# Block attention with a gated MLP: another order for the first 60 steps, and two tiles' low parts on another engine

## The chip, the core and the metric

The kernel runs on one core of one Trainium2 chip. The metric is the device time of one execution in microseconds (us), the median of several runs. A core has a matrix engine (TensorE, PE in the rows; its weight loads are PEld), a vector engine (VectorE, DVE), an engine for activation functions (ScalarE, ACT), a general engine (GpSimd, POOL) and SyncE (SP), which here issues the DMA transfers. Each engine works through its own instructions in order; semaphores tie the engines together.

## What is computed

There are 8 batches of 576 tokens, 8 heads of width 64. Attention stays inside chunks of 64 tokens. Its result, laid out as 512 features for each token, goes into an MLP whose second half of hidden features is normalised, mixed over the tokens by a 576x576 matrix and multiplied onto the first half:

```python
scores = scale * np.matmul(q_c, k_c.transpose(0, 1, 2, 4, 3))      # chunks of 64 tokens
attn = np.exp(scores - max); attn = attn / (sum + 1e-09)
x = np.matmul(attn, v_c)                                           # -> (8, 576, 512)
h = gelu_tanh(x @ w_in)                                            # 512 -> 1024
u, v = h[..., :512], h[..., 512:]
v_n = (v - mean) / np.sqrt(var + 1e-06) * g_ln
v_s = np.einsum('ts,bsd->btd', w_sg, v_n) + b_sg[None, :, None]
out = x + (u * v_s) @ w_out
```

## The kernel before

**Numbers in two parts.** The MLP's products are taken as high part times high part plus the two cross terms, so each operand of the MLP exists as a high and a low tile: `xh`/`xl` for x, `win_h`/`win_l` for w_in, and so on. An element of w_in arrives as a 64-bit word and has to be turned into such a pair on the chip. `pair_begin` does the first half on ScalarE and VectorE: one ScalarE pass (L130) and five VectorE passes (L131, L132, L133, L162, L166) for 512 columns. `pair_end` does the second half: ScalarE writes the high part (L174), four TensorE products with small diagonal matrices add up what is left in PSUM (L178), and ScalarE writes the low part (L179). w_in has eight such parts: four for the v columns (one for each 128 input features) and four for the u columns. The loads of the u parts go into the same staging tiles as the v parts', so `v_w_end` issues each of them when its v part is done.

**Attention tiles.** The 4608 tokens are 36 tiles of 128 rows. A tile is loaded (`att_load`), its scores are made on TensorE (L314 for tiles 0 to 4, L322 for later ones), VectorE takes the maxima (L333), then either ScalarE makes the exponentials head by head with the maximum as its bias (L344, tiles 0, 2 and 4) or VectorE subtracts and ScalarE makes one pass (L346, L349). The sums are inverted on VectorE (L356, L357) and multiplied on (L358): on VectorE for the first batches' tiles, but on GpSimd where the step's name, here `n2`, stands in the table `ON_POOL`. The first five tiles are transposed on TensorE (L366) and copied out by ScalarE (L368); the product with V is L398. `keep` then writes that result into `xf`, `xh` and `xl`. For a tile whose name (`l0` to `l3`) is in `ON_POOL`, ScalarE copies PSUM to `xf` (L428), casts `xf` to `xh` (L94), and GpSimd subtracts (L97). For any other tile ScalarE casts PSUM to `xh`, VectorE subtracts from PSUM (L97), and ScalarE copies `xf` last (L432). For the first tile of a batch 64 of its rows are copied once more into `xodd` (L438).

**MLP units.** For a batch, `v_unit` (L452, 12 matmuls of 512 columns; five units for two batches together, four otherwise), four `u_unit` (L489), four `s_unit` (the mixing over tokens, L509) and four `o_unit` (L532) follow each other. After the first two batches they run in a fixed loop, with the attention of the next batch put into slots between them.

**The order of the start.** Everything up to the end of batch 1 is written in the string `START` (L46 to L50), one word a step: A loads tiles up to a number, S, T and O are a tile's scores, transpose and product (P and Q two tiles at once), L, W and w load, begin and end a v part of w_in, X and x begin and end a u part, M and G load other constants, g splits w_sg, v, u, s and o are the units (v03 is unit 3 of batch 0), and D with a number makes that many spare matmuls (`keep_clock`, L577) that nothing uses. The framework's scheduler sets each engine's queue from this program order and from the dependencies, so a queue is close to the order of the string but not the same word for word. PSUM has three tiles for scores, units and parts (`ps_m`) and two banks which the transposes and products of the first tiles take in turn (`next_bank`).

Of the kernel before, what the change touches and what calls it, by code (L numbers as in the profile page):

```python
# [42 lines left out]


START = """
L0 A0 A1 L1 S0 L2 T0 D11 A2 W0 A3 W1 L3 A4 S1 W2 S2 w0 w1 W3 T1 O0 w2 S3 O1 T2 w3 D14 O2 T3 S4 M0 v00 X0 O3 G0 T4 v01  # L46
A8 O4 x0 X1 v02 x1 X2 v03 X3 v04 u00 x2 g0 g1 u01 x3 g2 g3 u02 P5 g4 u03 T5 s00 T6 P7 s01 Q5 s02 T7 T8 s03 Q7 v10 v11
Y0 v12 Y1 v13 Y2 u10 Y3 u11 Y4 u12 Y5 Y6 u13 Y7 A10 s10 A12 s11 P9 s12 s13 T9 o00 T10 P11 o01 o02 o03 Q9 A14 T11 o10
T12 o11 Q11 S13 A15 o12 T13 o13
"""  # L50

PE_TILES = 5
# [9 lines left out]
}  # L62


ON_POOL = ("l0", "l1", "l2", "l3", "n2")
ACT_SOFTMAX = (0, 2, 4)


# [12 lines left out]
def block_attention_gated_mlp(ctx: ExitStack, tc: tile.TileContext, qkv, w_in, w_out, w_sg, g_ln, b_sg, out):  # L81
# [41 lines left out]
    def pick(step):  # L123
        return nc.gpsimd if step in ON_POOL else nc.vector

# [292 lines left out]
    def keep(t, xo):  # L418
        for b, at, off, n in segments(t):
# [6 lines left out]
            dst = [a[b][:, :, off : off + n].rearrange("p hp (c s) -> p c hp s", s=D) for a in (xh, xl, xf)]  # L426
            if f"l{t}" in ON_POOL:
                nc.scalar.copy(dst[2], src)  # L428
# [208 lines left out]
```

## Time and profile before

| what | value |
|---|---|
| median of 3 runs (lowest, highest) | 514.78 us (514.69, 514.84) |
| the profiled execution's own time | 516.12 us |
| its span, from first to last instruction | 514.3 us |
| mean granted TensorE clock | 0.996 of full |
| TensorE busy | 500.4 us, 97% of the span |
| VectorE, ScalarE, GpSimd busy | 337.0, 274.4, 73.7 us |
| TensorE in the chain that ended last | 83% of the span |

The profile is one execution. Its busy times tell how full an engine is, and its chain follows the last instruction back through whatever released it. A single share over 514 us hides that the start works under other limits than the rest: in the first 40th of the span TensorE is busy at 5 tenths, in nearly all later ones at 9 or more. So the first 70 us are read instruction by instruction, in the timeline.

### The profile page before, as it was taken

How to read it: one execution, taken by the hardware profiler on the slowest of the kernel's cores; microseconds unless marked ns; L12 is line 12 of the kernel's file. 1: busy time of each engine (PE TensorE's matmuls, PEld its weight loads, DVE VectorE, ACT ScalarE, POOL GpSimd, SP SyncE). 2: the span in 40 equal slices, each digit the busy share in tenths (PEclk: the TensorE clock that was granted, in tenths of full speed). 3: DMA queues.
4: the chain of work that ended last, by engine and by line, in shares of the span. 5: the costliest groups of instructions: out<-in, count | busy, mean ns of one | idle time of the engine just before them, and what ended most of it. 6: DMA issues, size and time to landing. Idle time of an engine off the chain costs nothing.

```text
span 514.3 us, 12454 instructions
## 1 busy us (share of the span) xinstructions
PE 500.4 (97%) x5273; PEld 464.8 (90%) x5278; DVE 337.0 (66%) x704; ACT 274.4 (53%) x509; POOL 73.7 (14%) x75
## 2 busy tenths in 40 slices
PE   5989999899999999999999999999999999999997
PEld 5677899699999899998999899998999899998996
DVE  5978759986866875577465686578456685536042
ACT  5788667853435865345643666345644666334210
POOL 0033300020110231013100140013100140102000
PEclk9999999899999999999999999999999999999999
DMA  8776001216438404060406304060406200020002
GB/s 333 271 217 198 0 1 43 70 38 174 114 113 222 138 1 126 24 193 2 124 4 190 87 0 126 24 192 2 124 1 193 86 0 3 14 81 0 1 1 92
DMA packets 49595, 46.58 MB, mean 91 GB/s; under 512 B 35202, under 2 KB 39554, under 8 KB 49540
## 3 DMA queue, kind: packets, MB, share of 16 engines
q1 hardware_dynamic: 49540, 45.80, 29.5%
q8 instruction: 41, 0.67, 0.5%
q14 instruction: 14, 0.11, 0.1%
HBM read 36.34 MB, written 9.44 MB: 89 GB/s over the span
## 4 chain that ended last, share of the span: by engine, by line
PE 83%; DVE 6%; ACT 5%; POOL 2%; issue 2%; DMA 1%; DVEq 0%; SPq 0%; POOLq 0%; ACTq 0%
PE pm L509 21%; PE pm L532 19%; PE pm L489 19%; PE pm L452 17%; PE pm L410 3%; PE banks L322 3%; POOL sm L461 1%; PE pm L577 1%; DMA qkv_t<-qkv 1%; DVE nmax L333 1%; PE pm L314 1%; ACT ptT L380 1%; ACT ptT L375 1%; POOL xl L97 1%; ACT pt L344 0%
## 5 line engine op out<-in xcount | busy, mean ns | idle before, releaser
L509 PE MATMUL pm<-wsg,v 128*128 128x288 f32 x768 | 108.0, 296 | 0.0
L509 PEld LDWEIGHTS pm<-wsg,v 128*128 128x128 f32 x768 | 103.9, 189 | 0.4
L532 PE MATMUL pm<-gh,wout 128*128 128x288 f32 x512 | 92.3, 297 | 0.0
L532 PEld LDWEIGHTS pm<-gh,wout 128*128 128x128 f32 x512 | 76.1, 189 | 0.5
L358 POOL TENSOR_TENSOR pt<-pt,den 128x512 f32<-128x512 f32 x28 | 30.8, 1112 | 226.3 <-DVE den L357 151.3
L461 POOL TENSOR_TENSOR sm<-sm,neg_half 128x1 f32<-128x1 f32 x36 | 36.3, 1008 | 160.4 <-DVE sm L460 120.1
L489 PE MATMUL pm<-xh,win_l 128*128 128x288 f32 x256 | 55.4, 298 | 0.7 <-ACT win_l L179 0.7
L532 PE MATMUL pm<-gl,wout 128*128 128x288 f32 x256 | 55.4, 296 | 0.0
L94 ACT CAST gh<-gt 128x576 fp32r<-128x576 f32 x32 | 21.5, 673 | 62.8 <-DVE gt L513 62.7
L489 PE MATMUL pm<-xh,win_h 128*128 128x288 f32 x256 | 55.0, 296 | 0.0
L489 PE MATMUL pm<-xl,win_h 128*128 128x288 f32 x256 | 55.0, 296 | 0.0
L452 PE MATMUL pm<-win_h,xl 128*128 128x512 f32 x128 | 52.0, 407 | 0.0
L452 PE MATMUL pm<-win_l,xh 128*128 128x512 f32 x128 | 51.2, 400 | 0.0
L452 PE MATMUL pm<-win_h,xh 128*128 128x512 f32 x128 | 51.1, 399 | 0.0
L513 DVE TENSOR_TENSOR gt<-pm,u 128x576 f32<-128x576 f32 x32 | 24.2, 756 | 40.2 <-PE pm L509 40.2
L540 DVE TENSOR_TENSOR ot<-pm,xf 128x576 f32<-128x576 f32 (+1 forms) x33 | 24.1, 733 | 29.8 <-PE pm L532 29.8
L489 PEld LDWEIGHTS pm<-xh,win_l 128*128 128x128 f32 x256 | 41.4, 188 | 2.2 <-ACT win_l L179 1.2
L532 PEld LDWEIGHTS pm<-gl,wout 128*128 128x128 f32 x256 | 41.5, 189 | 0.0
L489 PEld LDWEIGHTS pm<-xl,win_h 128*128 128x128 f32 x256 | 41.1, 188 | 0.0
L489 PEld LDWEIGHTS pm<-xh,win_h 128*128 128x128 f32 x256 | 41.0, 188 | 0.0
L97 DVE TENSOR_TENSOR xl<-pm,xh 128x512 fp32r<-128x512 f32 (+1 forms) x34 | 21.8, 640 | 26.2 <-ACT xh L94 26.2
L458 DVE BATCH_NORM_STATS2 sm<-hs 128x6 f32<-128x512 f32 x36 | 24.8, 688 | 19.6 <-ACT hs L455 19.4
(121 smaller groups left out, 830.8 us busy)
## 6 DMA issues: line engine op xcount, KB each, us to landing
qkv_t<-qkv SPq DMA_DIRECT2D x32, 512.0 KB, 4.5
out_dram<-ot SPq DMA_DIRECT2D x31, 288.0 KB, 2.2
qkv_t<-qkv SPq DMA_DIRECT2D x124, 64.0 KB, 3.6
qkv_t<-qkv SPq DMA_DIRECT2D x3, 768.0 KB, 9.7
wsg<-w_in SPq DMA_DIRECT2D x4, 512.0 KB, 5.2
wout<-w_in SPq DMA_DIRECT2D x4, 512.0 KB
st<-w_out SPq DMA_DIRECT2D x8, 256.0 KB, 3.1
stage<-w_sg SPq DMA_DIRECT2D x5, 288.0 KB, 3.6
```

Of the source, the lines that this page charges most:

```text
L94: nc.scalar.copy(hi, src)
L97: lo_eng.tensor_tensor(lo, src, hi.bitcast(F32), op=ALU.subtract)
L322: nc.tensor.matmul(sc[o, c, h // 2, :], qt[r, 0, h, :], qt[r, 1, h, :], start=True, stop=True)
L358: (nc.gpsimd if t > last[1] else pick(f"n{t}")).tensor_tensor(pt, pt, den.unsqueeze(2).broadcast_to([P, H, D]), op=ALU.mult)
L452: nc.tensor.matmul(pv, a[:, kt, tok], c[:, kt, DH:], start=(i == 0), stop=(i == 11))
L458: nc.vector.bn_stats(st, h)
L461: nc.gpsimd.tensor_tensor(rs, rs, neg_half, op=ALU.pow)
L489: nc.tensor.matmul(pm[:, j, :HS], a[:, kt, dc], c[:, kt, j * HS : (j + 1) * HS], start=(i == 0), stop=(i == 11))
L509: nc.tensor.matmul(pm[:, j, :HS], a[:, dc], c[:, m, j * HS : (j + 1) * HS], start=(i == 0), stop=(i == len(ops) - 1))
L513: nc.vector.tensor_tensor(gt.rearrange("p (a c) -> p a c", a=2), pm[:, :, :HS], u2[0][:, dt, :].rearrange("p (a c) -> p a c", a=2), op=ALU ...
L532: nc.tensor.matmul(pm[:, j, :HS], a[:, kt, ec], c[:, kt, j * HS : (j + 1) * HS], start=(i == 0), stop=(i == len(ops) - 1),)
L540: nc.vector.tensor_tensor(ot[:, js], pm[:, js, :HS], res[:, js], op=ALU.add)
```

## The change

The string `START` is written anew in its first third, and three names leave `ON_POOL`; nothing else is touched.

```diff
 START = """
-L0 A0 A1 L1 S0 L2 T0 D11 A2 W0 A3 W1 L3 A4 S1 W2 S2 w0 w1 W3 T1 O0 w2 S3 O1 T2 w3 D14 O2 T3 S4 M0 v00 X0 O3 G0 T4 v01
-A8 O4 x0 X1 v02 x1 X2 v03 X3 v04 u00 x2 g0 g1 u01 x3 g2 g3 u02 P5 g4 u03 T5 s00 T6 P7 s01 Q5 s02 T7 T8 s03 Q7 v10 v11
+L0 A0 L1 A1 L2 L3 A4 W0 S0 W1 D8 w0 S1 W2 T0 w1 S2 O0 T1 W3 w2 S3 O1 T2 M0 w3 S4 O2 T3 v00 X0 O3 G0 T4 v01 x0 X1 O4 A8
+v02 x1 X2 v03 X3 v04 u00 x2 g0 g1 u01 x3 g2 g3 u02 P5 g4 u03 T5 s00 T6 P7 s01 Q5 s02 T7 T8 s03 Q7 v10 v11 Y0 v12 Y1
...
-ON_POOL = ("l0", "l1", "l2", "l3", "n2")
+ON_POOL = ("l0", "l1")
```

The loads of the v parts 1 to 3 (L1, L2, L3) are issued ahead of those of tiles 2 to 4 (before, part 3 came behind tile 3). The v parts are begun and ended earlier between the tiles' steps. Of the spare matmuls 8 stay of 25: D11 becomes D8, D14 goes. Units v00 and v01 keep their words but stand differently to the steps around them. The low parts of tiles 2 and 3, and the multiplication that ends the softmax of tile 2, move from GpSimd to VectorE. From the gelu of u01 on, every engine's queue is the same as before.

On TensorE, from the first scores on, before (`qkv_t_108` and `qkv_t_111` are tiles 0 and 1, `wsg_0_106` is the staging tile of v part 0):

```order
L314 MATMUL pm_115<-qkv_t_108 64x64 x16
L577 MATMUL pm_156<-ident_84 128x128 x11
L314 MATMUL pm_188<-qkv_t_111 64x64 x16
L366 MATMUL banks_105<-ident_84,pt_134 128x128 x4
L314 MATMUL pm_221<-qkv_t_168 64x64 x16
L178 MATMUL pm_254<-wsg_0_106,ident_84 128x512
```

and now (`qkv_t_113` is tile 1, `wsg_1_111` is v part 1):

```order
L314 MATMUL pm_131<-qkv_t_108 64x64 x16
L577 MATMUL pm_170<-ident_84 128x128 x8
L178 MATMUL pm_179<-wsg_0_106,ident_84 128x512
L178 LDWEIGHTS low_0_86
L178 MATMUL pm_179<-wsg_0_106,low_0_86 128x512
L178 LDWEIGHTS low_1_87
L178 MATMUL pm_179<-wsg_0_106,low_1_87 128x512
L178 MATMUL pm_179<-win_h_90,ident_84 128x512
L314 MATMUL pm_188<-qkv_t_113 64x64 x16
L366 MATMUL banks_105<-ident_84,pt_150 128x128 x4
L178 MATMUL pm_227<-wsg_1_111,ident_84 128x512
```

Three spare matmuls are gone, and part 0's four products stand in front of the scores of tile 1; part 1's follow the transpose of tile 0.

On TensorE just ahead of the first matmul of v00 (L452), before (`pt_240` is tile 2, `pt_338` tile 3, `qkv_t_168` tile 2, `qkv_t_186` tile 4):

```order
L577 MATMUL pm_380<-ident_84 128x128 x5
L366 MATMUL banks_105<-ident_84,pt_240 128x128 x4
L577 MATMUL pm_380<-ident_84 128x128 x9
L398 MATMUL banks_105<-ptT_369,qkv_t_168 64x64 x16
L314 MATMUL pm_420<-qkv_t_186 64x64 x15
L366 MATMUL banks_105<-ident_84,pt_338 128x128 x4
L314 MATMUL pm_420<-qkv_t_186 64x64
L452 MATMUL pm_454<-win_h_90,xl_302 128x512
```

and now (`pt_255` is tile 2, `qkv_t_123` tile 4, `wout_1_117` part 3):

```order
L178 MATMUL pm_369<-wout_1_117,low_1_87 128x512
L314 MATMUL pm_378<-qkv_t_123 64x64 x13
L366 MATMUL banks_105<-ident_84,pt_255 128x128 x4
L314 MATMUL pm_378<-qkv_t_123 64x64 x3
L178 MATMUL pm_369<-win_h_90,ident_84 128x512
L452 MATMUL pm_436<-win_h_90,xl_287 128x512
L452 MATMUL pm_436<-win_l_91,xh_286 128x512
L398 MATMUL banks_105<-ptT_366,qkv_t_119 64x64 x16
```

The fourteen spare matmuls are gone, v00 begins in front of the product of tile 2 (the last row), and the transpose of tile 3 has moved into v01.

On ScalarE around the exponentials of tile 2, before (`pt_240`, in L344) with part 3's high part behind them (`wout_1_184`):

```order
L368 COPY ptT_282<-banks_105 128x512
L344 ACTIVATE pt_240,den_241<-pm_221,nmax_238 128x64 x8
L428 COPY xf_300<-banks_105 128x2x4x64
L179 ACTIVATE win_l_91<-pm_310 128x512
L94 CAST xh_301<-xf_300 128x2x4x64
L174 ACTIVATE win_h_90<-wout_1_184 128x512
L438 CAST xodd_0_306<-xh_301 128x4x64
L438 CAST xodd_1_307<-xl_302 128x4x64
L349 ACTIVATE pt_338<-pt_338 128x512
L428 COPY xf_300<-banks_105 128x2x4x64
L179 ACTIVATE win_l_91<-pm_371 128x512
```

and now (`pt_255` is tile 2, `pt_335` tile 3):

```order
L174 ACTIVATE win_h_90<-wout_0_115 128x512
L428 COPY xf_285<-banks_105 128x2x4x64
L94 CAST xh_286<-xf_285 128x2x4x64
L438 CAST xodd_0_291<-xh_286 128x4x64
L179 ACTIVATE win_l_91<-pm_307 128x512
L438 CAST xodd_1_292<-xl_287 128x4x64
L368 COPY ptT_299<-banks_105 128x512
L344 ACTIVATE pt_255,den_256<-pm_236,nmax_253 128x64 x8
L428 COPY xf_285<-banks_105 128x2x4x64
L349 ACTIVATE pt_335<-pt_335 128x512
L94 CAST xh_286<-xf_285 128x2x4x64
```

The copies and casts of tile 0 and its wait for `xl` have moved in front of tile 2's exponentials; the copy of tile 1 (`xf_285`, second time) follows directly behind them.

## Rows read from the trace of the kernel before

**Rows 1.** Stretches: us, PE, PEld, DVE, ACT, POOL busy, granted clock, DMA, GB/s.

```profile
15.00:20.00 5.00, 4.60 (x18) 2.10 (x15) 5.00 (x13) 3.52 (x6) 0.00 (x0) 1.00 0.77 279
20.00:25.00 5.00, 5.00 (x82) 3.28 (x83) 4.85 (x12) 4.58 (x21) 0.33 (x1) 1.00 0.65 196
```

**Rows 2.** Chain that ended last, first 35 us: start, us, engine, tile, line.

```profile
5.74 1.98 PE pm L314 x32
7.71 4.64 PE pm L577 x22
12.35 1.10 PE pm L314 x32
13.48 0.69 DVE nmax L333
...
24.67 1.04 POOL pt L358
25.71 1.25 POOL xl L97
```

**Rows 3.** Timeline of PE: start, us, instruction; in brackets idle before, and releaser.

```profile
28.54 0.63 PE L366 MATMUL banks<-ident,pt 128*128 128x128 f32 x4 [0.82 <-ACT xf L428]
...
29.00 2.17 PE L577 MATMUL pm<-ident 128*128 128x128 f32 x18
...
34.66 0.50 PE L452 MATMUL pm<-win_h,xl 128*128 128x512 f32 x1
...
65.06 0.53 PE L489 MATMUL pm<-xh,win_l 128*128 128x288 f32 x2 [0.74 <-ACT win_l L179]
```

**Rows 4.** Timeline of PE: part ends, a product, v and u units.

```profile
15.03 1.12 PE L178 MATMUL pm<-wsg,ident 128*128 128x512 f32 x2
...
16.66 1.02 PE L178 MATMUL pm<-wsg,ident 128*128 128x512 f32 x2
...
24.66 1.15 PE L398 MATMUL banks<-ptT,qkv_t 64*64 64x64 f32 x32
...
44.77 0.40 PE L452 MATMUL pm<-win_h,xl 128*128 128x512 f32 x1
...
47.57 1.02 PE L178 MATMUL pm<-wsg,ident 128*128 128x512 f32 x2
...
59.43 0.43 PE L489 MATMUL pm<-xh,win_l 128*128 128x288 f32 x2
...
62.62 1.02 PE L178 MATMUL pm<-wout,ident 128*128 128x512 f32 x2
```

**Rows 5.** Timeline of DVE and ACT: softmax of tiles 1, 2, part 3.

```profile
18.62 0.68 DVE L358 TENSOR_TENSOR pt<-pt,den 128x512 f32<-128x512 f32 x1
...
20.83 0.42 DVE L131 TENSOR_SCALAR wout<-wout 128x512 f32<-128x512 f32 x1
20.95 0.31 ACT L344 ACTIVATE pt<-pm,nmax 128x64 f32<-128x64 f32 x1
...
22.93 0.69 DVE L166 SCALAR_TENSOR_TENSOR wout<-wout 128x512 uint16<-128x512 uint16 x1
...
23.29 0.62 ACT L428 COPY xf<-banks 128x512 f32<-128x512 f32 x1
```

**Rows 6.** Timeline: POOL and DVE side by side, then DVE alone.

```profile
42.23 1.53 POOL L97 TENSOR_TENSOR xl<-xf,xh 128x512 fp32r<-128x512 f32 x1 [6.44 <-ACT xh L94]
...
42.60 1.70 DVE L467 SCALAR_TENSOR_TENSOR hs<-hs,sm,g_bc 128x512 f32<-128x512 f32 x1
...
48.05 0.74 DVE L467 SCALAR_TENSOR_TENSOR hs<-hs,sm,g_bc 128x512 f32<-128x512 f32 x1
```

**Rows 7.** Timeline of PE, and one stretch (columns of Rows 1).

```profile
81.65 1.16 PE L410 MATMUL pm<-ptT,qkv_t 64*64 64x64 f32 x64
...
91.94 1.94 PE L410 MATMUL pm<-ptT,qkv_t 64*64 64x64 f32 x64 [1.47 <-ACT ptT L380]
...
95.00:96.00 1.00, 1.00 (x4) 0.81 (x3) 1.00 (x4) 0.27 (x1) 0.00 (x0) 0.50 0.82 250
```

More of the change, by code (lines that the diff above doesn't have):

```diff
@@ L45 @@
 START = """
-L0 A0 A1 L1 S0 L2 T0 D11 A2 W0 A3 W1 L3 A4 S1 W2 S2 w0 w1 W3 T1 O0 w2 S3 O1 T2 w3 D14 O2 T3 S4 M0 v00 X0 O3 G0 T4 v01
-A8 O4 x0 X1 v02 x1 X2 v03 X3 v04 u00 x2 g0 g1 u01 x3 g2 g3 u02 P5 g4 u03 T5 s00 T6 P7 s01 Q5 s02 T7 T8 s03 Q7 v10 v11
-Y0 v12 Y1 v13 Y2 u10 Y3 u11 Y4 u12 Y5 Y6 u13 Y7 A10 s10 A12 s11 P9 s12 s13 T9 o00 T10 P11 o01 o02 o03 Q9 A14 T11 o10
-T12 o11 Q11 S13 A15 o12 T13 o13
+L0 A0 L1 A1 L2 L3 A4 W0 S0 W1 D8 w0 S1 W2 T0 w1 S2 O0 T1 W3 w2 S3 O1 T2 M0 w3 S4 O2 T3 v00 X0 O3 G0 T4 v01 x0 X1 O4 A8
+v02 x1 X2 v03 X3 v04 u00 x2 g0 g1 u01 x3 g2 g3 u02 P5 g4 u03 T5 s00 T6 P7 s01 Q5 s02 T7 T8 s03 Q7 v10 v11 Y0 v12 Y1
+v13 Y2 u10 Y3 u11 Y4 u12 Y5 Y6 u13 Y7 A10 s10 A12 s11 P9 s12 s13 T9 o00 T10 P11 o01 o02 o03 Q9 A14 T11 o10 T12 o11 Q11
+S13 A15 o12 T13 o13
 """
```

## The prediction, made before the changed kernel ran

> **What bounds the kernel now.** I read the stretches first. From 15 to 25 us VectorE is busy for 9.85 of 10 us [rows 1]: the start is bound by the softmax of the first tiles and the making of w_in's parts, both of which pass through VectorE. The chain of waits says the same with more detail. It runs through the 22 spare passes (4.64 us) into the scores of tile 1, from their end at 13.45 into VectorE (the maxima at 13.48), and about eleven us later into GpSimd, which does tile 2's multiplication and then the low part of tile 0 [rows 2]. Next I read TensorE's own timeline. The transpose of tile 2 waits until 28.54 for ScalarE, 18 more spare passes take 2.17 us behind it, and the first matmul of v00 starts at 34.66 [rows 3]. From there TensorE is nearly full, up to a last wait of 0.74 us at 65.06, the first matmul of u02 [rows 3]; from u01 on all queues are the same in both kernels. So the question is only when u02 starts: 65.06 us now. What comes behind is carried along, and 1 us earlier there is 1 us less of time.
>
> **Prices.** The end of a weight part takes TensorE 1.63 us (16.66 less 15.03), a product of one tile 1.15, a v unit 2.80 (47.57 less 44.77), a u unit 3.19 (62.62 less 59.43) [rows 4]; a transpose is 0.63 [rows 3], scores 1.10 [rows 2]. From tile 1's maxima at 13.48 [rows 2] to the end of its multiplication at 19.30 [rows 5] VectorE needs 5.82 us, with seven steps of weight parts between. The five VectorE steps of one part take 2.79 (20.83 to 23.62), and the exponentials of tile 2 keep ScalarE 2.34 (20.95 to 23.29) [rows 5]. A low part costs GpSimd 1.25 at the least [rows 2] and 1.53 at most [rows 6].
>
> **The change, step by step, up to v00.**
> 1. D11 to D8. Scores of tile 0 end at 7.71 as before. 22 passes in 4.64 us are 0.21 each; 16 are 3.37, so they end at 11.1 in place of 12.35: a gain of 1.25.
> 2. Part 0 ends in front of tile 1's scores: 1.63 more, and some 0.4 of it because TensorE is still slow there (0.21 us a pass, against 0.12 for the 18 later ones; tile 0's scores 1.98, tile 1's 1.10 [rows 2, 3]). So these scores run from 13.1 to 14.2, against 13.45 now: a loss of 0.75. In return VectorE has done the five steps of part 1 (2.79) while it would have waited. Part 1's load now stands in front of tile 1's on SP, and parts 2 and 3 in front of tile 2's; the chain holds no load behind 5.74 and the scores of tile 1 come later than now, so I cost the new order of loads at nothing. Had tile 1's load no time to spare, its size would be the price: half a tile's more, below 2 us. The u parts' loads are issued at the end of v parts, and these come earlier for parts 0 to 2.
> 3. Softmax of tile 1. Between its maxima and its multiplication stand seven weight steps now as before, so 14.25 + 5.82 = 20.1, 0.8 later. But behind it three steps of part 3 are left in place of all five and the rest of part 2: its last VectorE step ends at about 22.5, not 23.62.
> 4. Tile 2's exponentials. Its maxima are ready at 21.3. ScalarE comes later: TensorE does the transpose of tile 0, the end of part 1, the product of tile 0 and the scores of tile 2 up to 14.2 + 0.63 + 1.63 + 1.15 + 1.10 = 18.7; then ScalarE needs three steps of 0.5 to 0.6 for tile 0, waits for GpSimd's low part (1.25) and makes two more short ones: free at 22.15. The exponentials run to 24.5, 1.2 later than now. Here the move of n2 pays: VectorE multiplies in 0.68 as soon as the sums are there, pt2 is ready at 25.8, and the transpose of tile 2 can follow at once at about 25.9, since ScalarE's wait for the low part of tile 0 (GpSimd, 25.71 to 26.96 [rows 2]) now lies ahead of the exponentials. Now it is at 28.54 [rows 3]: a gain of 2.6.
> 5. v00 needs the low part of tile 1. Behind the exponentials ScalarE copies tile 1, makes tile 3's exponentials and the cast: 26.1. GpSimd adds 1.25 to 1.53: **v00 starts at about 27.5**, 7.2 earlier. The fourteen spare matmuls (2.17 for the second nine of them) have no place left in which they could cost anything.
>
> **From v00 to u02.** The stretch from 34.66 to 65.06 is 30.4 us, of which 0.74 is the last wait [rows 3], so 29.7 is work with small waits in it. v00 now starts with less done: the product of tile 2 (1.1, as the neighbours overlap) and the transpose of tile 3 (0.46 from 28.54 to what follows at 29.00 [rows 3]) come behind it. That makes 31.2. The last wait is gone: ScalarE writes u part 2's low half ahead of the normalised odd rows now. New waits come instead:
> - v01 needs the low part of tile 2, now on VectorE (three more steps of 0.69 there with n2 and tile 3). ScalarE makes tile 4's exponentials (2.34, from 28.3) ahead of tile 2's cast, so cast 31.2 and low part 32.3, while TensorE is through with v00 and one product at 31.3: **1.0 of waiting**. VectorE's subtraction alone is 0.7 of that; done on GpSimd it would be at least 1.25, so the move itself is no loss.
> - v02 waits in the same way for tile 3: 0.35.
> - GpSimd's two remaining low parts now run beside a busy VectorE. L467 took 1.70 us beside GpSimd's subtraction and 0.74 alone [rows 6]; so such a meeting costs between 0 and 0.96. One of the two falls into slack; for the other I take 0.3, nearer to nothing because most steps that it meets read PSUM.
>
> That makes 1.65 of new waits, and u02 starts at 27.5 + 31.2 + 1.65 = 60.35, or **4.7 us earlier** than 65.06. VectorE's work from tile 1's maxima to the end of the start grows by three steps of 0.69 and loses 2.79 done earlier, so it does not grow. The profiled execution took 516.12 for a span of 514.3; its span becomes 509.6, its time 511.4. Against the median, 514.78, the same 4.7 give **510.1 us**. The bound on the good side: no new waits at all, 1.65 less, 508.4.
>
> **A rule weighed against this.** After TensorE had stood for 1.47 us, the next product took 1.94 us, against 1.16 for the same at full clock, and the granted clock read 0.50 in the stretch at 95 us [rows 7], its level of 1.2 GHz in place of 2.4. A wait of 0.82 did not do that: the 18 spare passes right behind it ran at 0.12 each [rows 3]. The new wait ahead of v01, 1.0, lies between the two. The Trainium skill, "TensorE: Matmul & The Clock Gate", section "Part 1: The HAM clock gate", says that "the default state is throttled, and activity releases the throttle", which speaks against taking spare matmuls away; the trace agrees as far as these rows go. If the removal alone let the clock fall, the time would be that of the last rival below, not the forecast's.
>
> **Rivals.**
> - *The clock falls ahead of v01* (15%). In the fall of the trace the product lost 0.8 and the matmuls in 3 us behind it, at half rate, about 1.5: 2.3. Later waits would swallow part of it. With 0.4 swallowed, 510.1 + 1.9 = 512.0. For it: 1.0 is nearer to 0.82 than to 1.47, but my 1.0 may be 1.5. The same time comes out if VectorE is the bound again and each of its three new steps (2.07) lands on v01 to v03.
> - *No waits* (7%): ScalarE and VectorE run ahead, 508.4.
> - *Nothing is won* (5%): v00 starts early, but its low parts come no sooner than now, so that 4.7 more of waits stand between v01 and v04. Against it: the casts that they wait for move with the exponentials, 3 us or more.
> - *Slower: the clock stays low through the start* (7%). With three fewer spare matmuls and gaps between part 0, tile 1 and part 1, TensorE might keep its slow rate. From 11.1 to 27.5 it has about 14.7 us of work (four part ends 6.5, four scores 4.4, two products 2.3, three transposes 1.5) and 1.7 of waits. A product's 1.94 against 1.16 [rows 7] is a factor of 1.67, so 9.8 more, less the 1.7 that it fills: v00 at 35.6, 8.1 later. The new waits behind v00 would be filled too: 510.1 + 8.1 - 1.65 = 516.6, slower by 1.8. It decides where more than about 12 of the 14.7 us of work run at the slow rate. Against it: TensorE works without a gap from 5.74 to beyond 13, as it does now, and behind that the scores of tile 1 took 1.10 against 1.98 [rows 2].
>
> **Chances.** The forecast as it stands, 509.1 to 511.1: 66%. With the rivals: faster by over 0.2% 88%, within it 5%, slower 7%; 0.2% is about what a measurement of this kernel can tell from no change. The range leaves out nothing above the first rival's 512.0 plus the upper bound of a meeting with GpSimd (0.7 more), and on the other side 508.4 less 0.2 for an earlier v00: 508.2 to 512.7. The likeliest case alone has 509.1 to 511.1.
>
> **What would show it.** v00's first matmul near 27.5 and u02's near 60.35 confirm the sum. Scores of tile 1 near 13.1 to 14.2 confirm steps 1 and 2; the transpose of tile 2 at 26 without a wait for ScalarE step 4; an idle of about 1 us ahead of v01 that ends with VectorE's L97 confirms the new wait. Wrong would be: a granted clock of 0.50 before 60 us, a wait on a load ahead of tile 1 or 2, a wait of more than 2 us ahead of v01 or v02, or a stretch behind 65 us that is longer than now.

## The result and the profile after

The changed kernel took 510.15 us in the median (509.68 to 510.48), the kernel before, run beside it, 514.81 (514.69 to 515.02): a ratio of 0.9898 with an interval of 0.9884 to 0.9911. The forecast was 510.1.

The timeline of TensorE in the changed kernel (start and duration in us, line, instruction; in brackets the idle time before it and what ended it) answers to [rows 2 and 3] and to the first row of [rows 7]:

```profile
5.64 1.98 PE L314 MATMUL pm<-qkv_t 64*64 64x64 f32 x32 [5.64 <-DMA qkv_t<-qkv]
7.57 3.78 PE L577 MATMUL pm<-ident 128*128 128x128 f32 x16
11.14 1.34 PE L178 MATMUL pm<-wsg,ident 128*128 128x512 f32 x2
...
13.09 1.15 PE L314 MATMUL pm<-qkv_t 64*64 64x64 f32 x32
...
25.66 0.63 PE L366 MATMUL banks<-ident,pt 128*128 128x128 f32 x4
...
27.26 0.50 PE L452 MATMUL pm<-win_h,xl 128*128 128x512 f32 x1 [0.17 <-POOL xl L97]
...
32.47 0.50 PE L452 MATMUL pm<-win_h,xl 128*128 128x512 f32 x1 [0.87 <-DVE xl L97]
...
60.40 0.43 PE L489 MATMUL pm<-xh,win_l 128*128 128x288 f32 x2
...
87.16 1.94 PE L410 MATMUL pm<-ptT,qkv_t 64*64 64x64 f32 x64 [1.45 <-ACT ptT L380]
89.04 0.50 PE L452 MATMUL pm<-win_h,xl 128*128 128x512 f32 x1
89.38 0.39 PE L452 MATMUL pm<-win_l,xh 128*128 128x512 f32 x1
```

The transpose of tile 2 (25.66) and v00 (27.26) stand without the waits of before, v01 (32.47) has the new wait for VectorE, and u02 (60.40) has no wait: 4.66 us earlier than 65.06 [rows 3], which is the whole difference of the medians. The profiled executions differ by more, 510.48 against 516.12, that is 5.64. The rest lies behind: from the first matmul of L322, which follows u02, to the end of the execution before has 447.68 (516.12 less 68.44) and the changed kernel 446.80 (510.48 less 63.68). The profiled execution of before had the low granted clock of [rows 7]; in this one the matmuls right behind 89 us start 0.233 apart on average and the clock is full:

```profile
90.00:92.00 2.00, 2.00 (x10) 1.59 (x10) 2.00 (x5) 1.03 (x4) 0.00 (x0) 1.00 0.55 177
```

(Stretch; busy time of PE, PEld, DVE, ACT, POOL; granted clock; DMA share; GB/s.)

VectorE in the same kernel, which answers to [rows 5]:

```profile
14.28 0.69 DVE L333 TENSOR_REDUCE nmax<-pm 128x8 f32<-128x512 f32 x1 [1.50 <-PE pm L314]
...
19.10 0.68 DVE L358 TENSOR_TENSOR pt<-pt,den 128x512 f32<-128x512 f32 x1
...
20.30 1.29 DVE L133 SCALAR_TENSOR_TENSOR wout<-wout 128x512 int32<-128x512 int32 x1
...
22.09 0.69 DVE L166 SCALAR_TENSOR_TENSOR wout<-wout 128x512 uint16<-128x512 uint16 x1
...
24.82 0.69 DVE L358 TENSOR_TENSOR pt<-pt,den 128x512 f32<-128x512 f32 x1
...
26.14 1.09 DVE L356 TENSOR_SCALAR den<-den 128x8 f32<-128x8 f32 x1
...
31.72 0.69 DVE L97 TENSOR_TENSOR xl<-banks,xh 128x512 fp32r<-128x512 f32 x1
```

and GpSimd beside it:

```profile
19.77 1.28 POOL L97 TENSOR_TENSOR xl<-xf,xh 128x512 fp32r<-128x512 f32 x1 [18.48 <-ACT xh L94]
25.93 1.27 POOL L97 TENSOR_TENSOR xl<-xf,xh 128x512 fp32r<-128x512 f32 x1 [4.88 <-ACT xh L94]
```

Tile 1's maxima come at 14.28 and its multiplication ends at 19.78, part 3's last step at 22.78, tile 2's multiplication at 25.51. Two steps of VectorE are long for what they are: L133 takes 1.29 (0.68 at 16.49) and L356, on 8 elements a partition, 1.09 (0.17 at 24.38). Both stand beside a subtraction of GpSimd.

### The profile page after: what moved, and what is told of

Its sections match the earlier page's. It is cut to its first block, busy times and chain, and to the rows that moved or that the text cites. A ratio compares the mean times of both kernels' runs of the same rounds, so it can differ in the third digit from the quotient of the medians.

```text
span 508.7 us, 12385 instructions
## 1 busy us (share of the span) xinstructions
PE 495.6 (97%) x5244; PEld 458.6 (90%) x5244; DVE 338.8 (67%) x707; ACT 274.4 (54%) x509; POOL 69.6 (14%) x72
## 4 chain that ended last, share of the span: by engine, by line
PE 88%; DVE 6%; ACT 4%; DMA 1%; issue 1%; POOL 0%; DVEq 0%; SPq 0%; ACTq 0%
PE pm L509 21%; PE pm L489 20%; PE pm L532 19%; PE pm L452 18%; PE banks L322 3%; PE pm L410 3%; PE pm L178 2%; ACT pt L344 1%; DMA qkv_t<-qkv 1%; PE pm L314 1%; PE pm L577 1%; DVE blocks L372 1%; ACT xh L94 1%; ACT L455 1%; DVE xl L97 1%
## 5 line engine op out<-in xcount | busy, mean ns | idle before, releaser
L358 POOL TENSOR_TENSOR pt<-pt,den 128x512 f32<-128x512 f32 x27 | 29.7, 1113 | 202.0 <-DVE den L357 128.0
L452 PE MATMUL pm<-win_h,xl 128*128 128x512 f32 x128 | 51.5, 402 | 1.5 <-DVE xl L97 0.9
L452 PE MATMUL pm<-win_l,xh 128*128 128x512 f32 x128 | 50.8, 397 | 0.0
L452 PE MATMUL pm<-win_h,xh 128*128 128x512 f32 x128 | 50.7, 396 | 0.0
L97 DVE TENSOR_TENSOR xl<-pm,xh 128x512 fp32r<-128x512 f32 (+1 forms) x34 | 21.7, 640 | 26.2 <-ACT xh L94 26.2
## 6 DMA issues: line engine op xcount, KB each, us to landing
qkv_t<-qkv SPq DMA_DIRECT2D x32, 512.0 KB, 4.6
qkv_t<-qkv SPq DMA_DIRECT2D x3, 768.0 KB, 11.1
wsg<-w_in SPq DMA_DIRECT2D x4, 512.0 KB, 5.6
wout<-w_in SPq DMA_DIRECT2D x4, 512.0 KB, 6.0
```

Source lines behind the costliest of these rows:

```text
L97: lo_eng.tensor_tensor(lo, src, hi.bitcast(F32), op=ALU.subtract)
L358: (nc.gpsimd if t > last[1] else pick(f"n{t}")).tensor_tensor(pt, pt, den.unsqueeze(2).broadcast_to([P, H, D]), op=ALU.mult)
L452: nc.tensor.matmul(pv, a[:, kt, tok], c[:, kt, DH:], start=(i == 0), stop=(i == 11))
```

## The experiments

All kernels, with the start of TensorE's first matmul of v00 and of L322 (scores of tiles 5 and 6, between u02 and u03) in the profiled execution:

| kernel | median (lowest, highest), us | ratio to before, interval | v00 | L322 |
|---|---|---|---|---|
| changed kernel | 510.15 (509.68, 510.48) | 0.9898 [0.9884, 0.9911] | 27.26 | 63.68 |
| E1 engine move alone | 513.79 (512.83, 513.96) | 0.9969 [0.9956, 0.9982] | 32.37 | 66.41 |
| E2 order alone | 514.55 (513.42, 515.13) | 0.9987 [0.9977, 0.9996] | 26.92 | 66.94 |
| E3 before without D14 | 514.76 (513.20, 515.38) | 0.9988 [0.9978, 0.9999] | 30.76 | 68.07 |
| E4 changed, no spares | 511.17 (510.67, 511.83) | 0.9924 [0.9909, 0.9939] | 27.75 | 64.20 |
| E5 changed, old loads | 512.48 (512.01, 513.08) | 0.9949 [0.9934, 0.9964] | 30.16 | 65.34 |
| E6 changed, n2 on GpSimd | 510.10 (509.80, 510.84) | 0.9904 [0.9889, 0.9919] | 27.41 | 63.41 |
| E7 changed, only l2 moved | 511.72 (510.32, 512.40) | 0.9929 [0.9906, 0.9952] | 26.88 | 63.92 |
| E8 changed, nothing on GpSimd | 512.20 (511.29, 512.44) | 0.9939 [0.9925, 0.9954] | 27.43 | 64.96 |
| E9 changed, tile 4 on VectorE | 513.72 (512.91, 514.09) | 0.9964 [0.9950, 0.9979] | 27.38 | 65.94 |
| E10 changed, part 0 behind | 512.22 (511.89, 512.62) | 0.9940 [0.9921, 0.9959] | 28.68 | 65.19 |
| E11 changed, D14 back | 511.49 (510.21, 512.38) | 0.9922 [0.9900, 0.9944] | 30.02 | 63.92 |
| E12 E7 with a filled wait | 512.49 (512.26, 513.41) | 0.9955 [0.9941, 0.9968] | 27.20 | 64.24 |

The column of L322 is the better measure of the start. Behind it an execution takes 446.8 to 446.9 where the granted clock stays high (the changed kernel, E1, E3, E4, E5, E10, by the profiled executions) and 0.5 to 0.9 more where it falls behind the product L410 near 87 to 92 us (before 447.68, E2 447.73, E7 447.70, E11 447.66, E8 447.30). Three have no such fall and are long all the same. E12 (448.25) has a longer wait, read below. E9 (447.78) and E6 (447.43) wait for a load of q, k and v in the middle of an L322 some 59 us behind the first, E6 for 0.42 and E9 for 0.67, and right behind it they are 0.65 and 0.91 later than the changed kernel, counted from L322; in E9:

```profile
124.93 0.69 PE L322 MATMUL banks<-qkv_t 64*64 64x64 f32 x32 [0.67 <-DMA qkv_t<-qkv]
```

The column holds the chance of one execution too. With the same instructions of TensorE ahead, sixteen spare passes took 3.78 us in the changed kernel and 2.94 in E5 (E2, E6 to E12 lie between), and tile 1's scores moved with them, so a difference of less than about 0.8 in this column need not come from the edit.

### Order and engines, one without the other: E1 and E2

E1 is the kernel before with the move alone, E2 the changed kernel with the old engines:

```diff
 E1, in the kernel before
-ON_POOL = ("l0", "l1", "l2", "l3", "n2")
+ON_POOL = ("l0", "l1")
 E2, in the changed kernel
-ON_POOL = ("l0", "l1")
+ON_POOL = ("l0", "l1", "l2", "l3", "n2")
```

> The old order of steps with only the three names taken out of ON_POOL. Theory (the order carries the gain): tile 2's multiplication leaves GpSimd, so the low part of tile 0 begins some 0.75 us sooner and the transpose of tile 2 comes at about 27.8 in place of 28.5; v00 stays behind ScalarE's run of four L130. 513.5 to 514.3 us, 0.5 to 1.3 below the kernel before. Rival (the move of engines carries it): 3 us or more below, 511.8 or less.

> The new order with the old ON_POOL: tiles 2 and 3's low parts and tile 2's multiplication back on GpSimd. Theory: v00 near 27.5 still, but the transpose of tile 2 later by 0.4 and v01 waits for a low part of 1.28 in place of 0.69, after a later cast: 510.7 to 511.7 us. Rival (the move of engines carries the gain): 513 or more.

The move alone gives 1.1 of the median (514.93 before, beside it, to 513.79), within the expected range. The rows give more: L322 stands 2.0 earlier than in before, and v00, which the theory had left in its place, 2.3. The two medians are not alike: three of E1's five executions have mean clocks of 0.995 to 0.996, but only six of before's twenty have one below 0.998. Executions with like clocks differ by 1.9 (512.83 and 513.18 against 514.88, the median of the other fourteen; 513.80 against 515.68 at the low clocks). So the move alone is worth nearer to 1.9, and the theory's reason for the 1.1, an unmoved v00, does not hold. The order alone gives 0.4, and my theory of 510.7 to 511.7 fell. v00 starts early, at 26.92; the loss comes after it. TensorE in E2:

```profile
31.18 0.66 PE L366 MATMUL banks<-ident,pt 128*128 128x128 f32 x4
34.08 1.75 PE L398 MATMUL banks<-ptT,qkv_u 64*64 64x64 f32 x32 [2.25 <-ACT ptT L368]
35.77 0.79 PE L452 MATMUL pm<-win_h,xl 128*128 128x512 f32 x1
36.36 0.63 PE L452 MATMUL pm<-win_l,xh 128*128 128x512 f32 x1
36.78 0.63 PE L452 MATMUL pm<-win_h,xh 128*128 128x512 f32 x1
...
63.55 0.53 PE L489 MATMUL pm<-xh,win_l 128*128 128x288 f32 x2 [1.18 <-ACT win_l L179]
```

and the stretch behind the wait:

```profile
36.00:38.00 2.00, 2.00 (x6) 1.52 (x7) 1.59 (x4) 2.00 (x4) 0.00 (x0) 0.55 0.50 119
```

With tile 2's low part on GpSimd (it runs there at 33.62, against 31.72 on VectorE in the changed kernel) the whole of v01 stands behind tile 3's product, in place of seven of its matmuls in front of tile 3's transpose. So TensorE has nothing between that transpose and that product, waits 2.25 for ScalarE, and then runs at a granted clock near one half: the product takes 1.75 instead of 1.15, and matmuls stand 0.43 apart instead of 0.23. The fall is not the main loss: the one execution of E2 with a mean clock of 0.999 took 513.42, still 3.3 more than the changed kernel.

A name in `ON_POOL` sets more than the engine. With it ScalarE copies to `xf` first and casts from there, and tile 2's cast stands behind a table load of 1.28 and v00's gelu; without it the cast comes first. ScalarE in E2, then in the changed kernel:

```profile
32.94 0.61 ACT L94 CAST xh<-xf 128x512 fp32r<-128x512 f32 x1
...
31.07 0.62 ACT L94 CAST xh<-banks 128x512 fp32r<-128x512 f32 x1
```

The cast accounts for 1.87 of the 1.90 by which the low part starts later; GpSimd's longer subtraction adds 0.59. No run moves the engine without the cast, so what follows is the worth of both together. It is more than their own microseconds, since they decide what the scheduler can put into a gap.

### Which of the three moved steps: E6, E7 and E8

```diff
 E6
-ON_POOL = ("l0", "l1")
+ON_POOL = ("l0", "l1", "n2")
 E7
-ON_POOL = ("l0", "l1")
+ON_POOL = ("l0", "l1", "l3", "n2")
 E8
-ON_POOL = ("l0", "l1")
+ON_POOL = ()
```

> The changed kernel with only tile 2's multiplication back on GpSimd (ON_POOL = l0, l1, n2). Theory (in the changed order this step alone decides little): GpSimd's 1.04 in place of VectorE's 0.69, tile 2's transpose waits about 0.7 for it, v00 and u02 later by no more than 0.5, time 510.1 to 510.8. Rival (the prediction's step 4: the move of this step is what brings tile 2's transpose 2.6 us forward): the transpose at 27 or later, time 511.7 to 512.8.

> The changed kernel with only the low part of tile 2 on VectorE; those of tiles 0, 1 and 3 and tile 2's multiplication on GpSimd (ON_POOL = l0, l1, l3, n2). Theory (the low part of tile 2 decides, since v01 can stand in front of tile 3's product only when it comes early): v01 begins ahead of tile 3's product, no wait above 1.1 us behind v00 and no granted clock below 0.9 before 60 us, u02 at 60.5 to 61.7, time 510.3 to 511.5. Rival (the three steps are needed together): a wait above 1.5 us in front of a product or v02 and a granted clock near 0.5 behind it, time 512.5 to 514.

> The changed kernel with all low parts on VectorE (ON_POOL empty), GpSimd idle in the start. Theory (two VectorE steps lengthened by 0.60 and 0.92 us beside GpSimd's subtractions, and 1.25 there against 0.69 here): VectorE does 1.4 more and loses 1.5 less, the low part of tile 1 comes some 0.6 sooner, v00 at 26.3 to 27.0, time 509.3 to 510.2. Rival (VectorE is the bound in the start, each step on it counts in full): v00 at 27.9 or later, waits of over 1 us for VectorE's L97, time 511.0 to 512.0.

E6: the multiplication of tile 2 is worth nothing by its place. TensorE waits for it ahead of the transpose, as expected,

```profile
25.88 0.66 PE L366 MATMUL banks<-ident,pt 128*128 128x128 f32 x4 [0.65 <-POOL pt L358]
```

but L322 stands 0.27 earlier than in the changed kernel and the median is 510.10. E7 differs from E2 by one name, the low part of tile 2, and L322 moves from 66.94 to 63.92: this step (engine and cast) carries 3.0 us of the 4.7 in the new order. Tile 3's low part on GpSimd costs a wait of 0.93 ahead of v02, since the subtraction took 2.49 there. The median of E7, 511.72, is 0.2 above the theory's range (0.8 above its middle); its one execution with a mean clock of 0.999 took 510.32, the three at 0.996 took 511.62 to 512.40. What they have in common is seen in the profiled one, in TensorE's timeline

```profile
41.15 0.50 PE L452 MATMUL pm<-win_h,xl 128*128 128x512 f32 x1 [0.93 <-POOL xl L97]
...
87.41 2.28 PE L410 MATMUL pm<-ptT,qkv_t 64*64 64x64 f32 x64 [1.46 <-ACT ptT L380]
89.61 0.79 PE L452 MATMUL pm<-win_h,xl 128*128 128x512 f32 x1
90.20 0.63 PE L452 MATMUL pm<-win_l,xh 128*128 128x512 f32 x1
90.63 0.63 PE L452 MATMUL pm<-win_h,xh 128*128 128x512 f32 x1
```

and in the stretch behind:

```profile
90.00:92.00 2.00, 2.00 (x6) 1.52 (x6) 2.00 (x5) 1.22 (x3) 0.00 (x0) 0.50 0.70 214
```

It is the same wait as in the changed kernel (1.45 there, 1.46 here), but here the clock fell and there it did not. E8 shows the other side: with all low parts on VectorE its queue is the bound, as the rival said, and the time is a little above the rival's 511.0 to 512.0, though v00 is not as late as its 27.9. v00 waits 1.31 for VectorE's L97, although a subtraction takes 0.69 there against 1.27 on GpSimd, and L322 comes 1.3 later.

### Loads, and part 0: E5 and E10

```diff
 E5
-L0 A0 L1 A1 L2 L3 A4 W0 S0 W1 D8 w0 S1 W2 T0
+L0 A0 A1 L1 L2 A3 L3 A4 W0 S0 W1 D8 w0 S1 W2 T0
 E10
-L0 A0 L1 A1 L2 L3 A4 W0 S0 W1 D8 w0 S1 W2 T0
+L0 A0 L1 A1 L2 L3 A4 W0 S0 W1 D8 S1 w0 W2 T0
```

> The changed kernel with the loads at the start in their old order (L0 A0 A1 L1 L2 A3 L3 A4, so parts 2 and 3 of w_in are loaded behind tile 2 and tile 3 again; the begun parts W0 and W1 and all else stay as changed). Theory (the prediction's step 2: the order of the loads is worth nothing): v00's first matmul within 0.4 us of 27.26, u02's within 0.4 of 60.40, time 509.8 to 510.7. Rival (the early loads carry a part of the gain, since the steps on w_in's parts come later and push the low part of tile 1 back): v00 at 28.3 or later, time 511.2 to 513.

(By the diff it is parts 1 and 3 that come behind tiles 1 and 3 in E5; part 2 keeps its place ahead of tile 2.)

> The changed kernel with the end of part 0 behind tile 1's scores again (w0 behind S1). Theory (the prediction's step 2: 0.75 us lost at tile 1's scores, and 2.79 us of part 1's VectorE steps done in the wait for them): the scores run from about 11.2 to 12.3, VectorE then has tile 1's softmax and part 1's five steps together, the last VectorE step of part 3 is at most 0.9 us later, v00 at 27.3 to 28.2, time 510.2 to 511.1. Rival (the place of part 0 is free, the loads alone bring the gain): v00 and u02 within 0.3 of 27.26 and 60.40, or sooner, time 509.5 to 510.2.

E5 fell on the rival's side: 512.48, v00 at 30.16. VectorE in E5:

```profile
11.83 0.17 DVE L356 TENSOR_SCALAR den<-den 128x8 f32<-128x8 f32 x1 [2.61 <-ACT pt L344]
12.04 0.20 DVE L357 RECIPROCAL den<-den 128x8 f32<-128x8 f32 x1
12.28 0.69 DVE L358 TENSOR_TENSOR pt<-pt,den 128x512 f32<-128x512 f32 x1
12.89 0.42 DVE L131 TENSOR_SCALAR wsg<-wsg 128x512 f32<-128x512 f32 x1
```

Part 1's first step comes at 12.89. In the changed kernel it is at 8.95, in the time in which VectorE here stands idle for 2.61 us:

```profile
8.95 0.42 DVE L131 TENSOR_SCALAR wsg<-wsg 128x512 f32<-128x512 f32 x1
```

Part 1's load lands at 9.6 in E5 (issued at 2.58, 7.0 to land) and at 7.7 in the changed kernel (2.11 and 5.6). ScalarE's first pass over it stands behind tile 0's exponentials in E5, at 11.65, and ahead of them in the changed kernel, at 7.83. So the order of the loads is what lets part 1 be worked on in the wait for tile 0's exponentials, and it is worth 2.3 us. Part 3's load, which moves too, was not tried apart.

E10 missed both expectations on the slow side (512.22). Part 1's five steps are done in the same wait there, and VectorE is even a little ahead (part 3's last step at 21.74 instead of 22.09), so my reason for a gain from part 0's place is not what is at work. The loss stands in TensorE's waits from v01 on (v00, 1.4 later, has the product of tile 2 ahead of it here):

```profile
32.96 0.50 PE L452 MATMUL pm<-win_h,xl 128*128 128x512 f32 x1 [1.22 <-DVE xl L97]
...
39.93 0.50 PE L452 MATMUL pm<-win_h,xl 128*128 128x512 f32 x1 [0.75 <-DVE sm L460]
...
42.98 1.15 PE L398 MATMUL banks<-ptT,qkv_t 64*64 64x64 f32 x32 [0.66 <-ACT ptT L368]
```

The first was 0.87 in the changed kernel, the others did not show there. The scheduler wrote the queues of all engines differently from tile 1 on; which of the moves makes these waits was not tried apart. E4, where part 0 stays in front of tile 1's scores, has the same three waits (1.15, 0.75 and 0.67, at 31.96, 38.94 and 41.98), so part 0's place is not the only thing that brings them.

### The spare matmuls: E3, E4 and E11

```diff
 E3, in the kernel before
-S3 O1 T2 w3 D14 O2 T3 S4 M0 v00
+S3 O1 T2 w3 O2 T3 S4 M0 v00
 E4, in the changed kernel
-W0 S0 W1 D8 w0 S1 W2 T0
+W0 S0 W1 w0 S1 W2 T0
 E11, in the changed kernel
-O1 T2 M0 w3 S4 O2 T3 v00
+O1 T2 M0 w3 D14 S4 O2 T3 v00
```

> The kernel before without its second group of 14 spare matmuls. Theory: the 2.17 us of them in front of tile 2's product cost up to 1.2 us there, but the transpose of tile 3 still waits for ScalarE's copy at 33.2 behind four L130, so v00 stays within 0.3 us of 34.66: 514.4 to 514.8 us. Rival (the spare matmuls carry the gain): 512.6 or less. Rival (they keep the clock up): a granted clock of 0.50 before 40 us and more than 515.5.

> The new order without any spare matmul. Theory: part 0 ends sooner, tile 1's maxima begin at 12 to 13 in place of 14.28 and everything behind moves with them by 1 to 2 us, if TensorE's rate rises at the same time as now: 508.3 to 509.3 us. Rival (low clock through the start): the matmuls of parts 0 and 1 and of tiles 1 and 2 keep the slow rate of 0.21 us a pass; v00 not before 29 and 512 us or more.

> The changed kernel with the fourteen spare matmuls (28 passes) back between the end of part 3 and tile 4's scores. Theory (without them TensorE has no idle time there that they could fill but 0.17 us, so they cost what they last): 28 passes of 0.12 are 3.4 us, less the 0.17 in front of v00 and the 0.87 in front of v01 that they fill, u02 2.0 to 2.4 later, time 512.1 to 512.6. Rival (spare passes slip into waits as they were meant to, or the clock they hold is worth it): 510.2 to 511.0.

E3's median was hit, for a wrong reason: v00 came 3.9 us earlier, at 30.76, not within 0.3 of its old place. The gain was lost at u02, in TensorE's timeline

```profile
63.17 0.53 PE L489 MATMUL pm<-xh,win_l 128*128 128x288 f32 x2 [1.85 <-ACT win_l L179]
```

and in the stretch behind it, where the clock fell:

```profile
66.00:68.00 2.00, 2.00 (x11) 1.91 (x9) 0.00 (x0) 0.00 (x0) 0.00 (x0) 0.58 0.00 0
```

From u02 to L322 E3 takes 4.90, before 3.38, so the fall costs 1.5 there; its lowest execution, 513.20 with a mean clock of 1.00, is 1.6 below before's 514.8. The low clock that the second rival had named came too, but behind a wait at 63 us and not before 40. E4 fell between the two expectations: taking the eight spare matmuls out saves nothing and costs 1.0 of the median (0.5 at L322). TensorE does not stay slow without them: the scores of tile 1 take 1.15 at 10.25 us already, 2.8 earlier than in the changed kernel. Part of that goes in waits for ScalarE ahead of v00 (0.35, 0.82, 0.60 and 0.41), the rest in the three waits named above. E11's 3.4 us of spare passes cost 0.24 at L322, not 2.0 to 2.4, and its lowest execution (510.21) is the changed kernel's time; the three others, at mean clocks of 0.995 to 0.996, took 511.39 to 512.38. TensorE has no wait in E11 from v00 to u02 that is longer than 0.11. In E11 ScalarE casts tile 2 ahead of tile 4's exponentials, in the changed kernel behind them, and so tile 2's low part is there before TensorE asks for it at 32.92; VectorE in E11:

```profile
31.22 0.68 DVE L97 TENSOR_TENSOR xl<-banks,xh 128x512 fp32r<-128x512 f32 x1
```

Besides, that execution's start was 0.67 us faster for no change of mine (16 spare passes 3.28 instead of 3.78). So the passes cost about 0.9 (0.24 and 0.67) in place of 3.4, and I had counted only the two waits that they fill.

### Taking the last wait away: E9

```diff
-ACT_SOFTMAX = (0, 2, 4)
+ACT_SOFTMAX = (0, 2)
```

> The changed kernel with tile 4's softmax in the form of tiles 1 and 3 (VectorE subtracts the maxima, ScalarE makes one pass; ACT_SOFTMAX = 0, 2). Theory (v01's wait of 0.87 us comes from tile 4's eight exponentials on ScalarE in front of tile 2's cast, as the prediction said): ScalarE is some 1.8 us sooner at that cast, the wait goes, u02 at 59.5 to 59.9, time 509.3 to 509.7. Rival (VectorE is as full as ScalarE there, and its two further steps of 0.69 each push the low parts of tiles 2 and 3 back): the wait stays or moves to v02, time 510.5 to 511.5.

The wait at v01 is gone, and the kernel is 3.6 us slower (2.3 of it at L322), outside both expectations. Later in ScalarE's queue there is a longer wait instead (TensorE):

```profile
61.02 1.13 PE L178 MATMUL pm<-wout,ident 128*128 128x512 f32 x2 [3.13 <-ACT u L496]
```

In E9 ScalarE makes the normalised odd rows (L474, L475) ahead of u00's gelu (L496, at 60.33), and waits 2.53 for GpSimd before them; in the changed kernel that gelu is at 55.27, ahead of them. The stretch behind the wait, at full clock:

```profile
62.00:64.00 2.00, 2.00 (x15) 1.80 (x14) 0.00 (x0) 0.60 (x1) 0.00 (x0) 1.00 0.00 0
```
A wait that one takes away in the middle of a scheduled start can come back elsewhere.

### The wait behind which the clock fell or not: E12

```diff
 in E7
-s03 Q7 v10
+s03 D6 Q7 v10
```

> The kernel with only tile 2's low part moved to VectorE (ON_POOL = l0, l1, l3, n2), with six spare matmuls (12 passes of 0.12 us) in front of the product of tiles 7 and 8 (D6 ahead of Q7), where TensorE waits 1.46 us for ScalarE in every kernel so far and the granted clock fell behind it in some executions only. Theory (that kernel's median of 511.72 beside its best run of 510.32 is this fall: the product 2.28 in place of 1.94 and about six matmuls 0.43 apart, 1.5 us): the spare passes lie inside the wait and cost nothing, no execution shows a mean granted clock below 0.998, and the median is 510.1 to 510.7. Rival (the spread has another cause, or the fall comes all the same): mean clocks of 0.996 as before and a median of 511.2 to 512.4.

TensorE in E12:

```profile
86.11 1.50 PE L577 MATMUL pm<-ident 128*128 128x128 f32 x12
87.73 1.94 PE L410 MATMUL pm<-ptT,qkv_t 64*64 64x64 f32 x64
...
97.30 0.50 PE L452 MATMUL pm<-win_h,xl 128*128 128x512 f32 x1 [1.83 <-ACT hs L455]
```

The spare passes lie in the wait, the product is not behind its place, and no fall follows. Four of five executions have mean clocks of 0.998 to 0.999, against one of four in E7; one is still at 0.996, which the theory had ruled out. The changed kernel, without spare passes there, has three of four at 1.00, so these counts do not show that the passes kept the clock. The theory's time fell as well: 512.49. The wait for ScalarE ahead of v12, 0.36 in the changed kernel, is 1.83 now. The spare matmuls take one of the three tiles of `ps_m` in turn, so all later units sit in another tile than before; that this is what makes the wait is argued, not shown.

## Why the prediction was right, and where it was right by luck

*Steps 1 to 5* hold by their numbers. The spare passes end at 11.35 by their row (11.1 forecast), tile 1's scores run from 13.09 to 14.24 (13.1 to 14.2), tile 1's multiplication ends at 19.78 (20.1), part 3's last step at 22.78 (22.5), ScalarE is free at 21.87 (22.15), tile 2's transpose starts at 25.66 (25.9), v00 at 27.26 (27.5). Some of this closeness is luck, since the same sixteen passes took 2.94 to 3.78 us from run to run.

Three of the reasons given for them do not hold.

- *"I cost the new order of loads at nothing."* It costs nothing, but step 2's return, part 1's 2.79 us done in VectorE's wait, is the loads' doing: without them 2.3 us are gone (E5). I booked that gain to part 0's place, which is worth 2.1 of the median by another way (E10).
- *"Here the move of n2 pays."* It does not (E6). The transpose came 2.9 us forward all the same. What is left is the second reason of the same step, and the trace bears it out: ScalarE's wait for the low part of tile 0 (0.30, up to 21.08) lies ahead of tile 2's exponentials (21.87) now.
- *"VectorE's subtraction alone is 0.7 of that; done on GpSimd it would be at least 1.25, so the move itself is no loss."* It is no loss, but I treated it as a matter of 0.6 us. With all three moves undone the order gains 0.4 of 4.7 (E2), and with tile 2's low part alone moved L322 is back within 0.3 of the changed kernel (E7).

*From v00 to u02* two terms were mis-sized and cancelled. The changed kernel's stretches (columns as above) give

```profile
27.26:40.00 12.74, 11.77 (x102) 8.16 (x102) 11.80 (x28) 12.05 (x33) 1.64 (x2) 1.00 0.57 162
40.00:60.40 20.40, 20.40 (x133) 15.77 (x131) 17.63 (x36) 15.61 (x30) 5.03 (x5) 1.00 0.48 128
```

TensorE is busy for 32.17 us, not 31.2, and idle for 0.97, not 1.65: 33.14 where I had 32.85. The work was short by 1.0 because I took a transpose and a product at what they add between full neighbours (0.46 and 1.1), while in this order they cut units in two: from start to start, waits left out, the matmuls of the v units take 15.36 here and the same ones 14.37 in the kernel before. Of the waits v01's was 0.87 (1.0 forecast), v02's did not show (0.35), and the meetings with GpSimd, priced at 0.3 of bounds 0 to 0.96, were 0.60 and 0.92 on VectorE (1.29 less 0.69, 1.09 less 0.17). My reason for the small price, that most steps which they meet read PSUM, does not hold for these two: neither L133 nor L356 does. The first falls ahead of v00 and into slack. The second does not: behind L356 comes tile 4's L340, for which ScalarE waits ahead of tile 4's exponentials,

```profile
28.74 0.31 ACT L344 ACTIVATE pt<-pm,nmax 128x64 f32<-128x64 f32 x1 [0.47 <-DVE nmax L340]
```

and behind those stands the cast that v01 waits for. So up to 0.47 of v01's 0.87 comes from this meeting, and the 1.0 forecast for v01 came out near for a reason that it did not contain. With v00 0.24 early the sum came out 0.05 late by the rows; that closeness is chance, the sign and the place of the gain are not.

*The clock.* I read the 1.94 us of L410 against 1.16 [rows 7] as the clock's doing. The changed kernel's row at 87.16 shows the same 1.94 with full clock behind it: the second tile's transposed weights come late within the product (its weight loads wait for ScalarE's copies L380, the last of which ends at 88.36). With the clock low from within the product it takes 2.28 to 2.38 (E7, E11, E8). So a fall there costs 0.5 to 0.9 to the end of the execution. In the start a fall cost 1.5 in E3 and, by the intervals behind E2's wait, about as much there. All are below the 2.3 in the first rival, whose 0.8 for the product was read from the wrong pair. The price is not settled closer: E7's executions differ by 1.3 to 2.1, while the changed kernel's one with a mean clock of 0.996 took 510.00, no more than the others. The factor of 1.67 in the slower rival came from the same pair; the pair that shows the level is 0.43 against 0.23 between matmuls. The rival itself was real: it is E2, with a wait of 2.25 in place of v01's 0.87.

On the rule that activity releases the throttle (the Trainium skill, "TensorE: Matmul & The Clock Gate", section "Part 1: The HAM clock gate"): the runs agree in E2 and E3, where the clock fell behind waits of 2.25 and 1.85, and E12, with spare work in a wait and no fall behind it in the trace, does not speak against it; E9, with 3.13 of waiting and full clock behind it, does not fit as simply. The runs do not make spare matmuls necessary at the start: E4 has none, and real work took their place.

## What to carry to other kernels

Price a reordering by what it lets the next queue do, not only by the steps it moves: here three parts (loads early, part 0 early, low parts on the quicker engine) had each to be there, and taking any one away lost 2 to 4 of the 4.7 us. Put the other way round: by executions with like clocks the engines alone give 1.9 and the order alone 1.5 (one execution of E2), and the rest comes only with both. A sum that comes out right is not yet a reason that is right; check its terms one by one, since two of mine were wrong by 1.0 and 0.7 in opposite directions. And before a difference of 1 us is put down to an edit, look whether the granted clock fell in one of the two executions at the same wait.

## What the runs showed of the hardware that was not expected

- A VectorE step that begins while GpSimd subtracts can be held until GpSimd has ended. L356 on 8 elements started at 26.14 and ended at 27.23, GpSimd's subtraction ended at 27.20; L133 started at 20.30 and ended at 21.59, 0.54 behind GpSimd's end at 21.05. That looks like waiting for the whole of GpSimd's instruction, not like sharing. It does not happen to every step. In E7 the second row below (and L132 behind it) keeps its usual time inside GpSimd's subtraction, and there it is the subtraction that takes 2.49 in place of 1.28:

```profile
38.60 2.49 POOL L97 TENSOR_TENSOR xl<-xf,xh 128x512 fp32r<-128x512 f32 x1 [3.40 <-ACT xh L94]
38.95 0.69 DVE L166 SCALAR_TENSOR_TENSOR wsg<-wsg 128x512 uint16<-128x512 uint16 x1
```

  The Trainium skill, "GPSIMD Engine Reference", section "1. Specifications", names contention with VectorE instructions in a two-port mode or with two SBUF inputs; L133 fits the second. L356, with one operand of 8 elements, would have to be the first, and no run here shows its mode.
- The same wait of 1.45 to 1.46 us ahead of L410 left the granted clock at 1.00 in the changed kernel and took it to 0.50 in E7 and in before. E7's four executions have mean clocks of 0.996 three times and 0.999 once. Nor does the length of a wait decide alone: 1.85 (E3) and 2.25 (E2) were followed by a granted clock below 0.6, 3.13 (E9) by 1.00.
- The time until TensorE runs at its upper speed at the start differs from execution to execution with the same instructions ahead: sixteen spare passes took 3.78 us in the changed kernel and in E9, 3.28 in E11, 2.94 in E5. The granted clock reads 1.00 there in all four, so only the pace of the passes shows it.
